# An attention and two feed-forward stages on one core: w3 kept as float32, lower parts of weights on VectorE, and two edits of order in the first attention steps

## Chip, cores and metric

The kernel runs on one core of one Trainium2 chip. The metric is the device time of one execution in microseconds. The time before is the median of three runs, 943.5 us (942.43 to 948.34).

## The reference

All arrays are float32. Attention has 4 batches of 8 heads, 576 positions and 64 columns; two feed-forward stages follow on 2304 tokens of width 512.

```python
scores = scale * np.matmul(q, k.transpose(0, 1, 3, 2))
cum = np.cumsum(np.maximum(s, 0.0), axis=-1)
bias = -(cum[:, :, :, None] - cum[:, :, None, :])
scores = np.where(causal, -1e9, scores + np.minimum(bias, 0.0))
attn = softmax(scores)
x = (attn @ v)                  # to (2304, 512)
h = x @ w_in                    # 512 -> 2048
x = (h - np.tanh(h)) @ w_out    # 2048 -> 512
a, b = x @ w1, x @ w2           # 512 -> 1024 each
out = ((a * b) @ w3) @ w_out2   # 1024 -> 1024 -> 512
```

## The kernel before

**Numbers in two parts.** Large products are made from float32 operands cut in two: `hi` is a cast to the format fp32r, `lo` the rest, `src - hi`, in the same format. A product takes three matmuls (hi hi, hi lo, lo hi; `mm3`, L113). `split` (L63) makes both parts: the cast by ACT (L64), the subtraction by POOL unless `lo` names another engine (L65). Weights arrive in another bit layout; `plain` (L84) puts them in order with three DVE instructions (L88, L91, L93) from the tile `raw` into `cvt`, two buffers each, and `convert` (L97) is `plain` and `split`.

**Order of the work.** TensorE's order is the order of the program. The instructions of all other engines, and SP's DMA issues, are put in order by a scheduler that simulates the kernel; each engine then takes its queue in that order, and an instruction that waits holds all behind it. `in_turn(i, behind)` (L80) orders `i` after `behind` on the same engine without a semaphore; `after_pe` adds a real wait.

**Stage 1 (0 to some 425 us): attention and the first half of the first feed-forward.** 32 pairs of heads go through a list of steps. `at(step, order, fn, p)` (L491) enters a function at a step; within a step functions run by `order`. Kind A is the first 256 positions of a pair of heads, kind B the other 320 in three units B1, B2, B3. The first eight pairs are batch 0 (`first`): four A, then four B. For a pair that begins at step k0, a unit's scores (PE) stand at its step k, `minimum` (DVE) and `exps` (ACT) at k+1, `transposes` (PE) and `evacuate` (the copy pf from PSUM, ACT) `lag` steps later, `products` (PE, the tile pv), then `invert`, `turn`, `store` (ACT copies rt, a DMA writes it), `spread` (two DMAs rb broadcast the reciprocals) and `finish` (L360): DVE multiplies pv by rb into `xy`, ordered behind `least[0]`, the last minimum that the program has so far. For the first four pairs `finish` stands at k0 + 10, `products` at k0 + 7. Their pv tiles take turns in two PSUM banks (L317), so pair 3's pv needs the bank that `finish` of pair 1 frees. Scores and transposes share five PSUM tiles `s` (`ps_a`); a tile comes free with the copy or the exponential that reads it. Small matmuls `spare` fill TensorE up to step 11.

The feed-forward generator `ffn` (L400) fills TensorE between attention steps, in nine blocks of 256 tokens. A block starts when `written` says that its rows are in `xy`; `cut_x` (L407) casts and subtracts the block's four column groups into `xhl`. `step_of` (L539 to L546) spreads the products of a block over the steps between its `avail` and that of the blocks after it. Beside this run `conversions` (L369), which makes the eight first groups of w_in and w_out (16 conversions, named win and wout), and from step 36 on `parked` (L383), which converts the other 16, and writes them to DRAM (`park`, L103, L106).

**Stage 2 (to some 622 us): the second half of that feed-forward** in blocks of 512 tokens, products hb and yb. Beside it `preparations` (L656) converts w1, w2, the second w_out and w3. Of w3's eight groups 6 and 7 stay on chip as hi and lo; six are written as hi and lo, 1 MB each, to `w3_d` (L688).

**Stage 3 (622 to 672 us): w3 times the second w_out,** eight groups of 24 products w3o in the order 6, 7, 4, 5, 0, 1, 2, 3 (L835). `fetch_w3` (L828) reads a parked group back into one of two buffers `park`. The loop also makes the operands of stage 4 (`need`, `weights`) and issues the first loads of its weights, S and A (`load_unit`, L782).

**Stage 4:** the products of w1, w2 and of the combined weights, in units of 384 columns.

Of the kernel before, what the change touches and what calls it, by code (L numbers as in the profile page):

```python
# [8 lines left out]
F32 = mybir.dt.float32  # L9
F32R = mybir.dt.float32r  # L10
BF16 = mybir.dt.bfloat16
U32 = mybir.dt.uint32
# [3 lines left out]
P = 128  # L16
# [3 lines left out]
DM = 512  # L20
# [3 lines left out]
NG = 8  # L24
BLK = 256
# [12 lines left out]
def tile_kernel(ctx: ExitStack, tc: tile.TileContext, qk, v, s, w_in, w_out, w1, w2, w3t, w_o2, outT):  # L38
    nc = tc.nc
# [12 lines left out]

    cum_d = dr.tile([NH, S], F32, tag="cum_d", name="cum_d")
    yp_d = dr.tile([P, NC, NT], F32, tag="yp_d", name="yp_d")
    w3_d = dr.tile([NG, P, 2, 2, DM], F32, tag="w3_d", name="w3_d")
    wf_d = dr.tile([2 * (NF - F1), P, 2, DM], F32, tag="wf_d", name="wf_d")
    wg_d = dr.tile([NG, P, 7, 2, 2 * P], F32, tag="wg_d", name="wg_d")
    wo_d = dr.tile([7, 2, P, 2, 2, 2 * P], F32, tag="wo_d", name="wo_d")
# [4 lines left out]
    def split(dst_hi, dst_lo, src, hi=None, lo=None):  # L63
        i = (hi or nc.scalar.copy)(dst_hi, src)  # L64
        (lo or nc.gpsimd.tensor_sub)(dst_lo, src, dst_hi.bitcast(F32))  # L65
        return i
# [30 lines left out]
    def convert(raw, name, w=None, lo=None, behind=None):  # L97
        t = plain(raw, name, behind)
        w = slot(name) if w is None else w
        split(w[:, 0, :], w[:, 1, :], t, lo=lo)  # L100
        return w

    def park(raw, name, dst, pool, behind):  # L103

        w = convert(raw, name, pool.tile([P, 2, DM], F32R, tag="park", name=f"park_{name}", bufs=1), behind=behind)
        nc.sync.dma_start(dst, w.bitcast(F32))  # L106

    def fetch(name, src):
# [14 lines left out]
    with ExitStack() as actx:  # L123
# [18 lines left out]

        REL = ((0, 0), (0, P), (1, 0), (1, 384), (0, 384))

        latest, least, last_exp, paces = [None], [None], [None], []
        PACED = 70

        def paced(i):
# [157 lines left out]
        def evacuate(p, j, e):  # L306
            pieces, pt, at = p.pf[j, e]

            pf = a2.tile([P, {"B1": 512, "B2": 416}.get(j, 384)], F32, tag=f"pf{0 if j == 'A' else j[1]}".replace("3", "0"), name=f"pf{p.n}_{j}_{e}")
            (nc.vector.tensor_copy if j == "B2" and not p.first else nc.scalar.copy)(pf[:, :at], pt[:, :at])  # L310
            p.pf[j, e] = pieces, pf, at

        def products(p, j):
# [55 lines left out]
        def conversions(fs):  # L369
            todo = [(d, f, src[f], f"{n}{f}") for f in fs for d, src, n in ((win, w_in, "win"), (wout, w_out, "wout"))]  # L370
            raws = []
            for m in range(2):
                raws.append(load_raw(*todo[m][2:], behind=latest[0]))
                yield
            for m, (d, f, src, n) in enumerate(todo):
                d[f] = convert(raws.pop(0), n, behind=least[0])
                if m + 2 < len(todo):
                    raws.append(load_raw(*todo[m + 2][2:], behind=latest[0]))
                yield
# [20 lines left out]
        def ffn():  # L400
            pend = []
            cut = {}

            def ready(blk):
                return blk < NB and all(written[b] >= min(S, (blk + 1) * BLK - S * b) for b in range(B))

            def cut_x(blk, lo):  # L407
                xs = cut.setdefault(blk, [])
                c, c0 = len(xs), blk * BLK
                x = f2.tile([P, 2, BLK], F32R, tag="xhl", name=f"xhl{blk}_{c}", bufs=6)  # L410
                split(x[:, 0, :], x[:, 1, :], xy[:, c, c0:c0 + BLK], lo=lo)
                xs.append(x)

            for blk in range(NB):
                c0 = blk * BLK
                while not ready(blk):
                    yield False
                while len(cut.get(blk, ())) < NC:
                    cut_x(blk, nc.vector.tensor_sub)
                xs = cut[blk]  # L420
                ys = []

                def add_y(f, gh, gl, end, ys=ys, blk=blk):
                    while f not in wout:
                        next(conv)
                    if f == 0:
                        ys.extend(ps_y.tile([P, 2, BLK], F32, tag=f"y{z}", name=f"y{z}_{blk}") for z in range(2))
                    for n, (z, x) in enumerate(((0, gh), (1, gh), (0, gl))):
                        for c in range(NC):
                            o = ys[c // 2][:, c % 2, :]  # L430
                            nc.tensor.matmul(o, wout[f][:, z, P * c:P * c + P], x,  # L431
                                             start=f == 0 and n == 0 and c % 2 == 0, stop=f == F1 - 1 and n == 2,
                                             skip_group_check=True)
                            if n == 1 and c == 1:
                                yield True
                    if f == F1 - 1:
                        after[1].append(end)

                def end_y(ys=ys, blk=blk, c0=c0):
                    for z in range(2):  # L440
                        yo = f2.tile([P, 2, BLK], F32R, tag="xhl", name=f"yo{z}_{blk}", bufs=6).bitcast(F32)
                        nc.scalar.copy(yo, ys[z])
                        nc.sync.dma_start(yp_d[:, 2 * z:2 * z + 2, c0:c0 + BLK], yo)

                for f in range(F1):
                    while f not in win:
                        next(conv)
                    late = written[B - 1] == S
                    ph = ps_a.tile([P, 512], F32, tag="s", name=f"h{blk}_{f}") if late else ps_h.tile([P, 512], F32, tag="h", name=f"h{blk}_{f}")
                    hh = ph[:, :BLK]  # L450
                    for c in range(NC):
                        pace[0] = mm3(hh, win[f], P * c, xs[c][:, 0, :], xs[c][:, 1, :], c == 0, c == NC - 1)
                        if c == 1:
                            yield True
                    t = f2.tile([P, BLK], F32, tag="th", name=f"th{blk}_{f}")
                    gh = f2.tile([P, BLK], F32R, tag="gh", name=f"gh{blk}_{f}", bufs=3)
                    gl = f2.tile([P, BLK], F32R, tag="gl", name=f"gl{blk}_{f}", bufs=3)

                    def tanh(t=t, hh=hh):
                        nc.scalar.activation(t, hh, AF.Tanh)  # L460

                    def rest(t=t, hh=hh, gh=gh, gl=gl, blk=blk):
                        nc.vector.tensor_sub(t, hh, t)  # L463
                        if blk < 2:
                            split(gh, gl, t)
                        else:
                            split(gh, gl, t, hi=nc.vector.tensor_copy, lo=nc.vector.tensor_sub)

                    after[0].append(tanh)
                    after[1].append(rest)  # L470
                    yield True
                    if len(pend) > late:
                        yield from pend.pop(0)
                    pend.append(add_y(f, gh, gl, end_y))
                    if f >= 3 and ready(blk + 1) and len(cut.get(blk + 1, ())) < NC:
                        cut_x(blk + 1, nc.vector.tensor_sub)
                    if blk == NB - 1 and f:
                        next(conv2, None)
                        next(conv2, None)
                    yield True  # L480
            for p in pend:
                yield from p
            yield True
            yield True
# [18 lines left out]
        for p in pairs:  # L503
# [18 lines left out]
            at(ke + 5, 2.4, turn, p)  # L522
            at(ke + 6, 1.2, store, p)
            at(ke + 6, 3.9, spread, p)
            fin = ke + lag + (5 if p.first and p.early else 3)
            at(fin, 2.6, finish, p)
            if p.hp == H // 2 - 1:
                avail.append((S * p.b + (BLK if p.early else S), fin))
# [122 lines left out]
    def load_w3(f, z):  # L651
        return load_raw(w3t[f, :, 4 * z:4 * z + 4].rearrange("p m c -> p (m c)"), f"w3_{f}_{z}", behind=pace[0])
# [3 lines left out]
    def preparations():  # L656
# [19 lines left out]
        for f in range(NG):  # L676
            if f == NG // 2:
                for m in range(NG):
                    convert(load_raw(w_o2[m], f"wo2_{m}", behind=pace[0]), f"wo2_{m}", wo2[m], lo=nc.vector.tensor_sub)
                    yield  # L680
            pk = wt.tile([P, 2, 2, DM], F32R, tag="park", name=f"w3p{f}", bufs=2)
            for z in range(2):
                convert(load_w3(f, z), f"w3_{f}_{z}", pk[:, z], lo=nc.vector.tensor_sub)
                yield
            if f in W3ORDER[:2]:
                kept[f] = pk
            else:
                nc.sync.dma_start(w3_d[f], pk.bitcast(F32))  # L688

    with ExitStack() as bctx:  # L690
        b2 = bctx.enter_context(tc.tile_pool(name="b2", bufs=2, reuse_waits="tile"))
# [135 lines left out]

    def fetch_w3(f):  # L828
        if f not in w3b:
            w3b[f] = wt.tile([P, 2, 2, DM], F32R, tag="park", name=f"w3b{f}", bufs=2)  # L830
            nc.sync.dma_start(w3b[f].bitcast(F32), w3_d[f])
        return w3b[f]

    ctx.enter_context(tc.manual_schedule(engines={mybir.EngineType.PE}))
# [221 lines left out]
```

## Time and profile before

| | |
|---|---|
| median of 3 runs | 943.5 us (942.43 to 948.34) |
| profiled execution | 942.7 us |
| its span, first to last instruction | 940.9 us |
| busy: PE, DVE, ACT, POOL | 914.4, 641.4, 452.6, 211.7 us |
| mean granted clock of TensorE | 0.995 |

The profile shows one execution. PE is TensorE's matmuls, PEld its weight loads, DVE VectorE, ACT ScalarE, POOL GpSimd, SP the engine that issues the DMAs. A tile is named by the program's name without its number, and Lnnn is the line. In a timeline a line has its start, its length, the engine, the line, the operation, the tiles and shapes, and in brackets the idle time of the engine just before and what ended it. The granted clock is a share of full speed: 1.00 is 2.4 GHz, 0.50 is 1.2 GHz.

### The profile page before, as it was taken

Reading aid. Unit: us, or ns where it says so; the run is one execution under the profiler, and the core shown is the slowest. Engines: PE = TensorE matmul, PEld = TensorE weight load, DVE = VectorE, ACT = ScalarE, POOL = GpSimd, SP = SyncE. Lnnn points to the kernel's source line nnn. Section 1 sums busy time; section 2 is a strip of 40 time slices with the busy share of each in tenths; the row PEclk is TensorE's granted clock in tenths of the full one; section 3 lists DMA queues with packets and bytes.
Section 4 is the critical chain, followed back from the end, with each engine's and each line's share of the span. In section 5 each row is a group of like instructions: output and inputs, shape, how many; then the busy total and the mean of one; then the engine's idle time right before and its main releaser. Section 6 shows DMA issues by size and latency. Waiting matters only on the chain.

```text
span 940.9 us, 16373 instructions
## 1 busy us (share of the span) xinstructions
PE 914.4 (97%) x6022; PEld 800.3 (85%) x6025; DVE 641.4 (68%) x1403; ACT 452.6 (48%) x1061; POOL 211.7 (22%) x210
## 2 busy tenths in 40 slices
PE   8889999899999999999999999998999999999998
PEld 4567777788888889998888888987899999999998
DVE  7677777787777866776999978763145747564555
ACT  4567887777776753323434433342123432433133
POOL 2245856666555410000000000000011111111100
PEclk9799999999999999999999999999999999999999
DMA  5655365535454423489687736258399877777774
GB/s 161 196 164 170 114 205 182 168 137 179 154 169 147 152 98 100 169 308 405 250 293 279 265 110 209 85 207 291 119 319 325 322 257 271 262 271 258 284 267 148
DMA packets 59072, 199.21 MB, mean 212 GB/s; under 512 B 6544, under 2 KB 21040, under 8 KB 53360
## 3 DMA queue, kind: packets, MB, share of 16 engines
q1 hardware_dynamic: 58992, 198.17, 60.8%
q8 instruction: 47, 0.77, 0.3%
q14 instruction: 33, 0.27, 0.1%
HBM read 151.86 MB, written 46.29 MB: 211 GB/s over the span
## 4 chain that ended last, share of the span: by engine, by line
PE 81%; DMA 7%; DVE 5%; ACT 3%; issue 2%; POOL 1%; SPq 1%; ACTq 0%; DVEq 0%; POOLq 0%
PE hb L117 10%; PE yb L117 10%; PE h L117 9%; PE W L861 9%; PE y L431 9%; PE oW L924 5%; PE Y L861 5%; PE s_B L229 4%; PE pv L327 4%; PE oY L924 4%; PE pt_B L301 3%; PE w3o L117 2%; DMA w3b<-w_d 2%; PE V L861 2%; DMA cb<-cum_d 2%
## 5 line engine op out<-in xcount | busy, mean ns | idle before, releaser
L117 PE MATMUL h<-xhl,win 128*128 128x256 f32 x864 | 120.6, 286 | 2.8 <-DVE xhl L65 1.9
L117 PEld LDWEIGHTS h<-xhl,win 128*128 128x128 f32 x864 | 105.8, 188 | 13.4 <-issue 4.3
L994 POOL TENSOR_TENSOR xy<-c,c 128x384 f32<-128x384 f32 x12 | 15.4, 1280 | 425.4 <-DVE c L983 425.4
L117 PE MATMUL hb<-x,win 128*128 128x512 f32 (+1 forms) x480 | 104.9, 367 | 0.0
L117 PEld LDWEIGHTS hb<-x,win 128*128 128x128 f32 x480 | 83.9, 188 | 15.0
L206 POOL TENSOR_SCALAR pr<-cb,cq 128x384 f32<-128x384 f32 (+1 forms) x48 | 90.8, 1904 | 22.8 <-DMA cb<-cum_d 14.3
L117 PE MATMUL yb<-ghb,wout 128*128 128x512 f32 (+1 forms) x320 | 95.6, 367 | 0.0
L431 PE MATMUL y<-gh,wout 128*128 128x256 f32 x576 | 85.2, 287 | 0.5 <-DVE gh L64 0.5
L290 ACT ACTIVATE pr<-pr,nm 128x128 f32<-128x128 f32 (+2 forms) x120 | 71.5, 598 | 19.0 <-DVE nm L268 18.9
L431 PEld LDWEIGHTS y<-gh,wout 128*128 128x128 f32 x576 | 72.5, 189 | 3.7 <-issue 2.0
L117 PEld LDWEIGHTS yb<-ghb,wout 128*128 128x128 f32 x320 | 58.2, 188 | 9.9
L117 PE MATMUL yb<-glb,wout 128*128 128x512 f32 (+1 forms) x160 | 58.4, 367 | 0.0
L301 PE MATMUL pt_B<-ident,pr 96*128 96x96 f32 (+1 forms) x384 | 51.4, 256 | 1.4 <-DVE cq L601 0.9
L268 DVE CUSTOM_DVE_ANT_0 pr<-s_B,pr 96x512 f32<-96x512 f32 (+1 forms) x72 | 44.1, 638 | 8.7 <-PE s_B L229 8.7
L431 PE MATMUL y<-gl,wout 128*128 128x256 f32 x288 | 45.1, 279 | 3.2 <-POOL gl L65 2.7
L301 PEld LDWEIGHTS pt_B<-ident,pr 96*128 96x128 f32 (+1 forms) x384 | 41.2, 143 | 5.7 <-issue 3.3
L463 DVE TENSOR_TENSOR th<-h,th 128x256 f32<-128x256 f32 x72 | 30.0, 417 | 22.3 <-ACT th L460 21.6
L310 ACT COPY pf_B<-pt_B 128x512 f32<-128x512 f32 (+2 forms) x72 | 35.8, 499 | 19.3 <-PE pt_B L301 19.3
L460 ACT ACTIVATE th<-h 128x256 f32<-128x256 f32 x72 | 26.8, 373 | 34.4 <-PE h L117 34.3
L872 ACT COPY s<-Y 128x384 f32<-128x384 f32 x24 | 11.6, 482 | 63.0 <-PE Y L861 60.5
L431 PEld LDWEIGHTS y<-gl,wout 128*128 128x128 f32 x288 | 38.3, 188 | 3.8 <-POOL gl L65 3.1
L64 ACT CAST ghb<-thb 128x512 fp32r<-128x512 f32 (+1 forms) x40 | 23.2, 579 | 35.2 <-DVE thb L725 34.5
(215 smaller groups left out, 2076.7 us busy)
## 6 DMA issues: line engine op xcount, KB each, us to landing
S<-wg_d SPq DMA_DIRECT2D x24, 1024.0 KB
wo<-wo_d SPq DMA_DIRECT2D x42, 512.0 KB
A<-wg_d SPq DMA_DIRECT2D x24, 768.0 KB
qk<-in_qk SPq DMA_DIRECT2D x16, 576.0 KB
raw_win<-in_w_in SPq DMA_DIRECT2D x16, 512.0 KB
raw_wout<-in_w_out SPq DMA_DIRECT2D x16, 512.0 KB
raw_w<-in_w SPq DMA_DIRECT2D x16, 512.0 KB
wg_d<-pks SPq DMA_DIRECT2D x8, 1024.0 KB
```

The source lines that it names most:

```text
L117: i = nc.tensor.matmul(ps, a, b, start=first and n == 0, stop=last and n == 2, skip_group_check=skip)
L206: nc.gpsimd.tensor_scalar(out=t[:pw, e, :w], in0=p.cb[:pw, e, :w], scalar1=c, scalar2=0.0, op0=ALU.add, op1=ALU.min)
L229: latest[0] = nc.tensor.matmul(ps[e][:PW[i], o:o + k1 - k0], w[r, 0, CH0[i]:CH0[i] + PW[i]], x[r, 1, k0:k1], start=z == 0 and (not p.first ...
L268: least[0] = nc.vector.tensor_tensor_reduce(out=t[:pw, k0:k1], in0=ps[:pw, o:o + k1 - k0], in1=t[:pw, k0:k1], scale=-0.125, scalar=nm[:pw, ...
L290: last_exp[0] = nc.scalar.activation(t[:pw, :], t[:pw, :], AF.Exp, bias=m, scale=-1.0, accum_out=p.sums[:pw, e, c:c + 1])
L301: nc.tensor.transpose(pt[:, at:at + pw], p.pr[i][:pw, e, KC0[kj]:KC0[kj] + P], ident[:pw, :pw])
L310: (nc.vector.tensor_copy if j == "B2" and not p.first else nc.scalar.copy)(pf[:, :at], pt[:, :at])
L327: nc.tensor.matmul(p.pv[D * e:D * e + D, c:p.nq], p.vs[:, e, kj], pf[:, beg:end], start=z == 0, stop=z == len(todo) - 1, skip_group_check= ...
L431: nc.tensor.matmul(o, wout[f][:, z, P * c:P * c + P], x, start=f == 0 and n == 0 and c % 2 == 0, stop=f == F1 - 1 and n == 2, skip_group_c ...
L463: nc.vector.tensor_sub(t, hh, t)
L861: i = nc.tensor.matmul(ps[:, :T], w[:, x, P * j:P * j + P], b[:, y, j], start=first and j == n == 0, stop=stop and j == 1 and n == 2, skip ...
L924: nc.tensor.matmul(ps[:, :T], w[:, a, q % 2, P * j:P * j + P], x[:, b, q], start=o in ("B11", "B21", "T1") and q == z == 0, stop=o in ("T4 ...
```

## The change

Four edits. (1) `w3_d` holds w3 in float32, half as large; a parked group is stored straight from the tile `cvt` and split when it is fetched, through a buffer `raw`. (2) `conversions` and `park` make the lower part on DVE; POOL made it before. (3) `finish` of the first four pairs stands one step later, at k0 + 11; `avail`, from which the first block's start is taken, moves with it. (4) The casts of the first block's `xhl` are ordered, on ACT, behind the last `evacuate` of a pair of batch 0 that the program has by then.

```diff
-    w3_d = dr.tile([NG, P, 2, 2, DM], F32, tag="w3_d", name="w3_d")
+    w3_d = dr.tile([NG, P, 2, DM], F32, tag="w3_d", name="w3_d")
...
     def park(raw, name, dst, pool, behind):
-        w = convert(raw, name, pool.tile([P, 2, DM], F32R, tag="park", name=f"park_{name}", bufs=1), behind=behind)
+        w = convert(raw, name, pool.tile([P, 2, DM], F32R, tag="park", name=f"park_{name}", bufs=1), lo=nc.vector.tensor_sub, behind=behind)
         nc.sync.dma_start(dst, w.bitcast(F32))
...
         def evacuate(p, j, e):
-            (nc.vector.tensor_copy if j == "B2" and not p.first else nc.scalar.copy)(pf[:, :at], pt[:, :at])
+            i = (nc.vector.tensor_copy if j == "B2" and not p.first else nc.scalar.copy)(pf[:, :at], pt[:, :at])
+            if p.first:
+                copied[0] = i
...
         def conversions(fs):
-                d[f] = convert(raws.pop(0), n, behind=least[0])
+                d[f] = convert(raws.pop(0), n, lo=nc.vector.tensor_sub, behind=least[0])
...
             def cut_x(blk, lo):
-                split(x[:, 0, :], x[:, 1, :], xy[:, c, c0:c0 + BLK], lo=lo)
+                in_turn(split(x[:, 0, :], x[:, 1, :], xy[:, c, c0:c0 + BLK], lo=lo), None if blk else copied[0])
...
-            fin = ke + lag + (5 if p.first and p.early else 3)
+            fin = ke + lag + (6 if p.first and p.early else 3)
...
     def preparations():
-            pk = wt.tile([P, 2, 2, DM], F32R, tag="park", name=f"w3p{f}", bufs=2)
+            if f in W3ORDER[:2]:
+                kept[f] = wt.tile([P, 2, 2, DM], F32R, tag="park", name=f"w3p{f}", bufs=2)
             for z in range(2):
-                convert(load_w3(f, z), f"w3_{f}_{z}", pk[:, z], lo=nc.vector.tensor_sub)
+                if f in kept:
+                    convert(load_w3(f, z), f"w3_{f}_{z}", kept[f][:, z], lo=nc.vector.tensor_sub)
+                else:
+                    nc.sync.dma_start(w3_d[f, :, z], plain(load_w3(f, z), f"w3_{f}_{z}"))
                 yield
-            if f in W3ORDER[:2]:
-                kept[f] = pk
-            else:
-                nc.sync.dma_start(w3_d[f], pk.bitcast(F32))
...
     def fetch_w3(f):
         if f not in w3b:
+            raw = cv.tile([P, 2 * DM], U32, tag="raw", name=f"raw_w3b{f}").bitcast(F32).rearrange("p (z c) -> p z c", z=2)
+            nc.sync.dma_start(raw, w3_d[f])
             w3b[f] = wt.tile([P, 2, 2, DM], F32R, tag="park", name=f"w3b{f}", bufs=2)
-            nc.sync.dma_start(w3b[f].bitcast(F32), w3_d[f])
+            split(w3b[f][:, :, 0], w3b[f][:, :, 1], raw, lo=nc.vector.tensor_sub)
```

## Rows read from the trace of the kernel before

**Rows 1.** Stretches of all engines: length, busy us (instructions), clock, DMA share, GB/s.
```profile
0.00:180.00 180.00, 165.04 (x1230) 119.76 (x1234) 131.26 (x358) 123.15 (x357) 95.46 (x106) 0.97 0.51 163
180.00:420.00 240.00, 238.11 (x2082) 210.94 (x2081) 178.32 (x515) 144.34 (x383) 85.14 (x81) 1.00 0.49 164
420.00:620.00 200.00, 200.00 (x991) 170.01 (x990) 160.32 (x292) 79.39 (x140) 0.00 (x0) 1.00 0.64 230
622.00:672.00 50.00, 44.84 (x197) 36.02 (x196) 22.16 (x30) 14.12 (x22) 0.00 (x0) 1.00 0.71 268
```

**Rows 2.** Waits of PE in the whole span: us, times, longest.
```profile
PE w3o L117 <- DMA w3b<-w_d: 5.2, 4, 2.8
PE y L431 <- POOL gl L65: 2.7, 2, 1.8
PE s_B L229 <- ACT rt L343: 2.5, 1, 2.5
```

**Rows 3.** Timeline of PE, 31 to 54 us.
```profile
31.37 0.55 PE L301 MATMUL pt_A<-ident,pr 128*128 128x128 f32 x3
34.42 2.28 PE L229 MATMUL s_B<-qk 64*128 64x384 f32 x8 [2.51 <-ACT rt L343]
...
38.37 1.55 PE L327 MATMUL pv<-pf_A,vs 128*64 128x256 f32 x8
...
50.48 0.51 PE L117 MATMUL h<-xhl,win 128*128 128x256 f32 x2 [1.43 <-DVE xhl L65]
...
51.27 1.06 PE L229 MATMUL s_B<-qk 64*128 64x384 f32 x8
...
53.10 0.21 PE L245 MATMUL s_B<-maskb,identb 128*96 128x64 bf16 x1
```

**Rows 4.** Timeline of ACT, 32 to 35 us.
```profile
32.06 0.41 ACT L64 CAST xhl<-xy 128x256 fp32r<-128x256 f32 x1 [3.52 <-DVE xy L364]
...
34.12 0.25 ACT L343 COPY rt<-pri 4x128 f32<-4x128 f32 x1
```

**Rows 5.** Timeline of DVE, 31 to 55 us.
```profile
31.61 0.43 DVE L364 TENSOR_TENSOR xy<-pv,rb 128x256 f32<-128x256 f32 x1 [2.30 <-DMA rb<-rd]
...
33.48 1.49 DVE L65 TENSOR_TENSOR xhl<-xy,xhl 128x256 fp32r<-128x256 f32 x1
...
54.65 0.16 DVE L261 TENSOR_SCALAR nm<-nm 96x2 f32<-96x2 f32 x1
```

**Rows 6.** Stretches around the low clock, columns as in rows 1.
```profile
0.00:34.40 34.40, 29.26 (x173) 16.06 (x176) 25.21 (x68) 15.70 (x55) 8.71 (x22) 1.00 0.57 170
34.40:44.60 10.20, 10.18 (x37) 6.30 (x38) 6.65 (x17) 4.67 (x16) 2.45 (x3) 0.50 0.59 200
44.60:60.00 15.40, 13.40 (x93) 9.71 (x92) 12.72 (x31) 10.25 (x30) 5.25 (x5) 1.00 0.60 190
```

**Rows 7.** Chain that ended last: start, us, what.
```profile
657.66 8.75 DMA w3b<-w_d
```

**Rows 8.** Timeline of all engines in the W3 stage.
```profile
621.04 0.68 SPq L789 DMA_DIRECT2D A<-wg_d  x1
...
660.48 5.72 PE L117 MATMUL w3o<-wo,w3b 128*128 128x512 f32 x24 [2.85 <-DMA w3b<-w_d]
```

**Rows 9.** Groups by line and shape: busy, mean ns, idle before and its releaser.
```profile
L206 POOL TENSOR_SCALAR pr<-cb,cq 96x512 f32<-96x512 f32 x24 | 50.2, 2100 | 0.0
...
L65 DVE TENSOR_TENSOR w3p<-cvt_w,w3p 128x512 fp32r<-128x512 f32 x16 | 10.9, 686 | 2.5 <-ACT w3p L64 2.4
...
L65 DVE TENSOR_TENSOR pks<-cs,pks 128x1024 fp32r<-128x1024 f32 x8 | 9.8, 1219 | 1.2 <-ACT pks L64 1.2
...
L64 ACT CAST pks<-cs 128x1024 fp32r<-128x1024 f32 x8 | 8.4, 1054 | 8.1 <-DVE cs L666 8.0
```

**Rows 10.** Timeline of POOL.
```profile
33.36 1.33 POOL L65 TENSOR_TENSOR win<-cvt_win,win 128x512 fp32r<-128x512 f32 x1 [7.86 <-ACT win L64]
...
164.52 1.93 POOL L65 TENSOR_TENSOR park_wout<-cvt_wout,park_wout 128x512 fp32r<-128x512 f32 x1 [4.94 <-ACT park_wout L64]
```

More of the change, by code (lines that the diff above doesn't have):

```diff
@@ L143, in tile_kernel @@
         REL = ((0, 0), (0, P), (1, 0), (1, 384), (0, 384))
-        latest, least, last_exp, paces = [None], [None], [None], []
+        latest, least, last_exp, copied, paces = [None], [None], [None], [None], []
         PACED = 70
```

## The prediction

> **What bounds the kernel now.** I read three views, from coarse to fine. First the stretches [rows 1]: TensorE (PE) is busy for 165.0 of the first 180 us, 238.1 of the next 240, 200.0 of 200 from 420 to 620, and 44.8 of 50 from 622 to 672, where W3 is multiplied. So the kernel is bound by TensorE, and only what ends a wait of TensorE, or raises its clock, counts: 15.0 us are idle before 180 us and 5.2 us in the W3 stage; VectorE (DVE) has 48.7 us idle before 180 us. Second, who ended TensorE's waits [rows 2]: the reload of w3b 5.2 us in four waits, gl made by GpSimd (POOL) 2.7 us in two, and one wait of 2.5 us for the copy rt by ScalarE (ACT). Third, the instructions around the waits. In the PE timeline [rows 3] pt_A ends at 31.92, and the scores s_B start only at 34.42, released by rt. The ACT timeline says why rt was late [rows 4]: a cast of xhl stood 3.52 us at the head of ACT for xy, made by DVE, and rt was behind it. The DVE timeline says why xy was late [rows 5]: the product with the spread reciprocals stood 2.30 us at the head of DVE for the transfer rb, and wrote at 31.61. After this stall the clock goes [rows 6]: from 34.4 to 44.6 us the granted clock is 0.50, TensorE's lower level of 1.2 GHz, where it was 1.00 before and is 1.00 after. The stall is paid twice, as wait and as half speed.
>
> In the W3 stage the chain [rows 7] shows a load of w3b that needs 8.75 us from issue to landing, the last of six. A reload is issued when the product two groups earlier has freed its buffer, so it has one group of products, 5.72 us [rows 8], to hide under; what is left over shows at 660.48, where TensorE stood 2.85 us for the load before the last one.
>
> **Part 1, W3 as float32.** The six parked groups are stored once, 512 KB each where hi and lo were 1 MB, and come back through the two raw buffers; then ACT casts and DVE subtracts. The nearest operations have the same 128x1024, the pair on pks: cast 1.05 us, subtraction 1.22 us [rows 9], 2.27 together. The buffer of the split frees as today, so 2.27 us must fit into 5.72: 3.4 us to spare. The load itself has a buffer of its own, free once the split two groups earlier is through: 2 x 5.72 - 2.27 = 9.2 us before its split is due, against 8.75 for twice the bytes. The first two can be issued before the stage begins, since the conversions have left the raw buffers by then. So the loads are hidden and the splits too; ACT and DVE are busy for 14.1 and 22.2 of the 50 us [rows 1] and get 6.3 and 7.3 more. I take -4.7 of the 5.2, with 0.5 left for a split that stands behind another cast. Bounds: -5.2, if all goes; +8.4, if all six splits were bare (6 x 2.27 - 5.2), far off, since 3.4 us of slack stand before each.
>
> The parking side loses 12 casts and 12 subtractions of 0.69 us [rows 9] between 420 and 620 us, at nothing: TensorE has no gap there. The cover also holds against the new dependence, a converted tile that is freed only when its store has landed: the same buffer is wanted two conversions later, and the landing of 1 MB took 8.75 us [rows 7]. Were the cover gone, DVE would stand in front of the tanh differences for that long; TensorE has two groups in hand before it notices. On SP six stores become twelve, behind other producers of the same step.
>
> **Part 2, the first four products a step on, and the casts behind copies.** The product of pair 1 is now issued behind the minimum of the next scores and no longer stands in front of it; the casts of the first block come after copies from PSUM, so rt and the pf copies no longer wait for xy. The 2.51 us go, and s_B starts at 31.9. What is late next: pair 3's pv uses the PSUM bank of pair 1's, so it must wait for that very product, which now follows the minimum of these scores. From the next pair's rows at full clock: s_B from 51.27 to 53.31, 2.04 us [rows 3]; its minimum ends at 54.81, 1.50 us behind [rows 5]; the product takes 0.43. So s_B ends at 33.9 and pv starts at 35.9, against 38.37 now: -2.4, with a new wait of 2.0 us. If the clock stays at 1.00, the 6.2 us from 38.4 to 44.6 that run at 0.50 shrink by half: -3.1. Together -5.5. Given back: four casts and subtractions of xhl, spread out so far, come in a row right before the first h. Today h waits 1.43 us there [rows 3]; I add 0.9, between nothing and twice 0.9. I take -4.6. Bounds: -6.9 if that wait goes too (5.5 + 1.4), and +0.5 if the clock falls all the same (first rival). Both bounds hinge on the clock: a wait of 1.43 us did not lower it, one of 2.51 did [rows 3, 6]; 2.0 lies between, and I lean to the shorter one since TensorE works on both sides of it. The start of the first block a step later spreads the same products over fewer steps: nothing.
>
> **Part 3, lower parts by VectorE.** 32 subtractions leave POOL, 1.33 us each [rows 10], and come to DVE at 0.69 [rows 9], each directly behind a cast by ACT; the like ones on w3p waited 2.5 us in 16, 0.16 each. After 180 us TensorE is busy for 238.1 of 240 and hides them. About 21 run before that, 16 of the conversions and some five parked: 21 x 0.85 = 17.9 us, into 48.7 us of idle DVE. What DVE holds up meanwhile are minima, tanh differences, and through them exponentials and copies. As TensorE waits for somebody 15.0 of 180 us, 8%, I let 8% through: +1.4. Against it POOL: the park subtraction at 164.52 held POOL for 4.94 us of waiting plus 1.93 of work in front of the causal mask and the bias [rows 10], and gl, queued behind these, made the longer of the two gl waits; I take a quarter of the 2.7 us, 0.6. Net +0.8. Bounds: -2.7 if both gl waits go and DVE hides all, +17.9 if nothing is hidden.
>
> One row shows VectorE and GpSimd in each other's way: a subtraction of xhl took 1.49 us from 33.48 [rows 5], where 0.69 is the time of one twice as wide [rows 9], while POOL subtracted from 33.36 to 34.69 [rows 10]. The Trainium skill, "SBUF — State Buffer", section "Who interferes with whom", states that a VectorE instruction with two SBUF inputs contends with a GpSimd instruction that reads SBUF, and that the first to start holds the shared ports for its whole length. By that rule the trace agrees, and the moved subtractions, which have two such inputs, are exposed to POOL's bias instructions. From rows: a bias instruction takes 2.10 us [rows 9], half of it 1.05, and POOL is busy for 95 of the 180 us [rows 1], 0.53; the nine of the 21 that run beside the bias, after 85 us, would lose 9 x 0.53 x 1.05 = 5.0 us of DVE time, of which 8% is 0.4: 935.4 by the rule, 935.0 without it.
>
> **Sum.** The profiled execution took 942.7 us, 0.8 under the median of the runs. 942.7 - 4.7 - 4.6 + 0.8 = 934.2, and with the 0.8 for a median 935.0.
>
> **Rivals.** First, the clock falls in the new wait of pv. For: it fell after 2.51 us, and 2.0 is nearer to that than to 1.43. Against: TensorE works until 33.9. Ten us at half speed from 35.9 end 4.0 us later than today's, so part 2 gives -2.4 + 2.0 + 0.9 = +0.5 in place of -4.6: 940.1.
>
> Second, the gain of part 2 is hidden later: ahead of 180 us other engines set the pace, and TensorE only waits elsewhere. For: 15.0 us of idle from many releasers. Against: the loads follow TensorE's own scores, so they shift with it. 942.7 - 4.7 + 0.8 + 0.8 = 939.6.
>
> Third, the first w3 loads aren't early: SP issues the last of four loads of S and A at 621.0 [rows 8], 3.5 MB in all, and if the raw loads come behind them the first split is late by about what a reload costs now, 3.0 us: 938.0.
>
> Fourth, better: both gl waits go and DVE hides its work: 935.0 - 0.8 - 2.7 = 931.5.
>
> Fifth, slower: DVE is the bound before 180 us. Place: 17 to 180 us, each subtraction at the head of DVE's queue waiting for its cast with minima behind it. Price 0.85 each, 17.9 in all, of which 1.4 is counted. To bring the time above 943.5 it needs 8.5 + 1.4 = 9.9 of the 17.9: it decides from 55% exposed; all of it gives 951.5, with the clock's fall 956.6. Against: DVE is idle for 27% of that time.
>
> **How the numbers follow.** A measurement of this kernel can tell about 1%, 9.4 us, from no change: below 934.1 is faster, above 952.9 slower. My case 0.48, its own range 931 to 938.5, with 0.23 of it under 934.1; clock falls 0.16; hidden later 0.08; late loads 0.07; better 0.13; DVE 0.08, of it 0.05 over 952.9. Faster 0.23 + 0.13 = 0.36; slower 0.05; the rest 0.59. The range reaches down past the fourth case to 930 and up past the first to 943.
>
> **What would show it.** Right: no wait for w3b, raw loads issued before the first w3 product, split below 3 us; s_B of the first B pair starting at 32 with a wait of about 2 us ahead of pv; granted clock 1.00 between 34 and 45 us; POOL idle until the first gl. Wrong: a clock of 0.50 anywhere after 30 us; TensorE's idle before 180 us still near 15 with DVE its commonest releaser; waits of w3 products for the split.

## The result, and the profile after

| | before | after |
|---|---|---|
| median | 945.2 us (9 runs, 936.99 to 948.34) | 933.1 us (9 runs, 932.31 to 939.26) |
| profiled execution | 942.7 us | 932.9 us |
| its span, mean granted clock | 940.9 us, 0.995 | 931.1 us, 0.996 |

The ratio is 0.990 with an interval of 0.9867 to 0.9934: faster by about 1%, which is just what a measurement of this kernel can tell. The 933.1 us are 1.9 under the forecast of 935.0 and inside its range; as a ratio to the 943.5 us that the forecast went by, it is 0.991. The nine runs lie in two groups, five from 932.3 to 933.1 at a mean granted clock of 0.996 and four from 937.5 to 939.3 at 0.989. (Lines are 2 to 4 higher in the kernel after: L329 was L327, L366 was L364, L833 is the new load of raw_w3b.)

First the stretches of the kernel after; the columns are those of [rows 1]. The W3 stage begins 4.9 us sooner, so its stretch is cut from 612.

```profile
0.00:180.00 180.00, 165.85 (x1265) 121.10 (x1266) 140.73 (x390) 125.29 (x365) 69.84 (x85) 0.98 0.53 170
180.00:420.00 240.00, 239.45 (x2091) 212.74 (x2091) 181.79 (x527) 142.28 (x377) 69.91 (x70) 1.00 0.49 166
612.00:662.00 50.00, 50.00 (x247) 42.55 (x246) 30.59 (x39) 20.98 (x31) 0.00 (x0) 1.00 0.53 189
```

TensorE is full in the W3 stage, where it stood 5.2 us. Up to 180 us it is hardly fuller than before (165.9 against 165.0), though DVE took over 9.5 us of work and POOL lost 25.6. The waits of TensorE (us in total, times, longest), to be read beside [rows 2]:

```profile
PE h L117 <- DVE xhl L65: 3.2, 1, 3.2
PE y L433 <- POOL gl L65: 2.5, 2, 1.4
...
PE pv L329 <- DVE xy L366: 1.5, 1, 1.5
...
PE W L865 <- DMA A<-wg_d: 1.0, 1, 1.0
```

The waits for w3b and rt are gone. The longest wait for xhl is 3.2 us where it was 1.43 [rows 3], the forecast wait of pv is there with 1.5 us, and gl costs nearly what it did. The timeline of TensorE from 31 to 48 us, to set beside [rows 3]:

```profile
31.66 1.43 PE L229 MATMUL s_B<-qk 64*128 64x384 f32 x8
...
35.54 0.87 PE L329 MATMUL pv<-pf_A,vs 128*64 128x256 f32 x8 [1.48 <-DVE xy L366]
...
42.23 0.58 PE L301 MATMUL pt_B<-ident,pr 128*128 128x128 f32 x4 [0.61 <-ACT pr L287]
...
43.67 0.43 PE L117 MATMUL h<-xhl,win 128*128 128x256 f32 x1 [0.46 <-ACT xhl L64]
47.31 1.01 PE L117 MATMUL h<-xhl,win 128*128 128x256 f32 x3 [3.21 <-DVE xhl L65]
```

The scores s_B start at 31.66 without a wait and pv at 35.54, 2.8 us sooner than before. Then the first products h wait 3.67 us in two pieces. Before, they began without a wait, and only the last two of the first twelve waited, the 1.43 us of [rows 3] (the timeline of the kernel before):

```profile
47.17 0.94 PE L117 MATMUL h<-xhl,win 128*128 128x256 f32 x6
```

The stretches around the new wait show what the granted clock did:

```profile
42.00:43.60 1.60, 0.90 (x5) 0.52 (x5) 0.37 (x2) 1.60 (x7) 0.00 (x0) 1.00 0.95 382
43.60:47.30 3.70, 0.43 (x1) 0.19 (x1) 3.21 (x7) 1.89 (x6) 0.00 (x0) 0.54 0.07 26
47.30:50.60 3.30, 3.29 (x13) 2.63 (x15) 3.30 (x7) 1.33 (x4) 0.00 (x0) 0.50 0.88 317
50.60:60.00 9.40, 8.62 (x59) 5.93 (x57) 6.91 (x22) 5.91 (x20) 0.74 (x1) 0.99 0.52 163
```

Closer, around the fall:

```profile
43.60:43.80 0.20, 0.13 (x1) 0.13 (x1) 0.00 (x0) 0.20 (x2) 0.00 (x0) 1.00 0.47 184
43.90:44.10 0.20, 0.20 (x1) 0.00 (x0) 0.01 (x1) 0.20 (x2) 0.00 (x0) 0.50 0.12 46
```

The clock falls to 0.50, the level of 1.2 GHz, at 43.9 us, while the first of these products (43.67 to 44.10) is still on TensorE. So it does not fall in the long wait but as that begins, behind waits of 0.61 and 0.46 us. It stays low through the long wait and through 3.3 us of full work behind it. The old stall with its low clock [rows 6] was exchanged for another wait and another low stretch, 10 us later; that the wait brought the low clock isn't shown here. Why xhl was late stands in the chain that ended last, of which these are the pieces from 39 us on (start, us, what):

```profile
39.04 5.02 DMA raw_win<-in_w_in
44.09 0.43 DVE cvt_win L88
44.51 0.60 DVE cvt_wout L91
45.11 0.60 DVE cvt_win L91
45.72 0.60 DVE cvt_wout L93
46.32 0.60 DVE cvt_win L93
46.92 0.35 DVE xhl L65
...
47.31 1.44 PE h L117 x5
```

The conversion of a weight that isn't needed yet stands at the head of DVE: it waits for its load until 44.09, five instructions of two conversions follow, and only then comes the subtraction of xhl that TensorE needs. On ACT the four casts were through by 44.5 us:

```profile
43.20 1.33 ACT L64 CAST xhl<-xy 128x256 fp32r<-128x256 f32 x4
```

To see where the time went, I read the start of some pairs' pv in the PE timeline (pairs counted from 0), that of w3o, and the span:

| | before | after | gained so far |
|---|---|---|---|
| pv of pair 3 | 38.37 | 35.54 | 2.8 |
| pv of pair 4 | 60.34 | 59.75 | 0.6 |
| pv of pair 14 | 176.11 | 172.29 | 3.8 |
| pv of pair 31 | 366.04 | 360.61 | 5.4 |
| first w3o | 622.35 | 617.49 | 4.9 |
| end of the span | 940.9 | 931.1 | 9.8 |

The first 2.8 us are given back to 0.6 by pair 4; 4.3 come between there and the W3 stage; 4.9 come behind it.

### The profile page after: what moved, and what is told of

The parts are those of the page before. It is cut to its first block, busy times and chain, and to the rows that moved or that the text cites. A ratio compares the mean times of both kernels' runs of the same rounds, so it can differ in the third digit from the quotient of the medians.

```text
span 931.1 us, 16354 instructions
## 1 busy us (share of the span) xinstructions
PE 911.1 (98%) x6025; PEld 799.0 (86%) x6025; DVE 650.4 (70%) x1429; ACT 449.1 (48%) x1055; POOL 170.9 (18%) x178
## 4 chain that ended last, share of the span: by engine, by line
PE 85%; DVE 5%; DMA 4%; ACT 3%; POOL 2%; issue 1%; SPq 0%; ACTq 0%; DVEq 0%
PE h L117 10%; PE hb L117 10%; PE y L433 9%; PE yb L117 9%; PE W L865 9%; PE oW L928 5%; PE Y L865 5%; PE w3o L117 5%; PE pv L329 4%; PE s_B L229 4%; PE oY L928 4%; PE pt_B L301 3%; PE V L865 2%; POOL pr L206 1%; PE s_A L229 1%
## 5 line engine op out<-in xcount | busy, mean ns | idle before, releaser
L117 PEld LDWEIGHTS yb<-ghb,wout 128*128 128x128 f32 x320 | 58.2, 188 | 10.2 <-ACT ghb L64 0.3
L218 POOL TENSOR_SCALAR_AFFINE_SELECT pr<-pr 128x256 f32<-128x256 f32 (+2 forms) x60 | 28.6, 495 | 98.3 <-issue 79.7
```

What stands on the lines that cost most here:

```text
L117: i = nc.tensor.matmul(ps, a, b, start=first and n == 0, stop=last and n == 2, skip_group_check=skip)
L218: nc.gpsimd.affine_select(out=dg, in_=dg, pattern=[[0, 2], [-1, w - c]], compare_op=ALU.is_ge, fill=-8e9, base=0, channel_multiplier=1)
```

## Experiments

Every kernel is compared with the kernel before on the same chip.

### Each part alone

`e1_w3` is the kernel before with edit 1 only (w3 in float32).

> The kernel before with part 1 alone (w3 stored as float32, split when fetched). My theory: the four waits for w3b (5.2 us) go whole, nothing else moves, so about 5 us under the kernel before (ratio 0.9945), TensorE busy for 50.0 of 50 us in the W3 stage, no wait for w3b. Rival (the early part carries the change, and the W3 stage only looks better because the operands of the next stage are ready sooner): ratio 1.00, a new wait of 3 us or more at the first products behind W3.

Measured: 940.2 us, ratio 0.9949 (0.992 to 0.9979). The profile has no wait for w3b and keeps the stall for rt, 2.8 us. By the ratio part 1 is worth 4.8 us.

`e2_steps` is the kernel before with edits 3 and 4 only:

```diff
-                split(x[:, 0, :], x[:, 1, :], xy[:, c, c0:c0 + BLK], lo=lo)
+                in_turn(split(x[:, 0, :], x[:, 1, :], xy[:, c, c0:c0 + BLK], lo=lo), None if blk else copied[0])
...
-            fin = ke + lag + (5 if p.first and p.early else 3)
+            fin = ke + lag + (6 if p.first and p.early else 3)
```

> The kernel before with part 2 alone (finish of the first four pairs a step later and the first block's casts behind the copies). My theory: pair 3's pv comes 2 to 3 us earlier, but the first h then waits 2 us or more for xhl and the clock falls there, so that little is left at the first pv of the B pairs (0.5 to 1.5 us) and at the end: ratio 0.997 to 1.000. Rival (the 3.8 to 5 us that the changed kernel has gained by 200 us are the shifted steps' own): about 5 us less, ratio 0.9945.

Measured: 950.9 us, ratio 1.0066 (1.0034 to 1.0098): slower. The pv of pair 3 starts 2.6 us sooner, that of pair 4 5.8 us later, and that of pair 31 6.8 later. Three timelines of this kernel, of PE, DVE and POOL, and its stretch from 40 to 60 us (columns as above) show why:

```profile
47.69 1.01 PE L117 MATMUL h<-xhl,win 128*128 128x256 f32 x3 [4.10 <-DVE xhl L65]
```

```profile
44.47 0.43 DVE L88 TENSOR_SCALAR cvt_win<-raw_win 128x512 uint32<-128x512 uint32 x1 [2.58 <-DMA raw_win<-in_w_in]
...
47.22 3.25 DVE L65 TENSOR_TENSOR xhl<-xy,xhl 128x256 fp32r<-128x256 f32 x3
```

```profile
47.43 1.35 POOL L65 TENSOR_TENSOR wout<-cvt_wout,wout 128x512 fp32r<-128x512 f32 x1 [6.55 <-ACT wout L64]
48.74 1.45 POOL L65 TENSOR_TENSOR win<-cvt_win,win 128x512 fp32r<-128x512 f32 x1
```

```profile
40.00:60.00 20.00, 14.38 (x55) 8.72 (x53) 13.42 (x30) 9.57 (x31) 3.64 (x3) 0.63 0.46 159
```

The wait is that of the kernel after, longer: DVE stood 2.58 us for the load, and three subtractions of xhl took 3.25 us while POOL subtracted weights from 47.43 to 50.19; in the kernel after, with POOL idle there, the same three took 1.09 (46.84 us). The granted clock is 0.63 from 40 to 60 us where it was 0.88 before; here it falls inside the wait, 1.6 us after its start at 43.6. What part 2 removes at 31 us it loses again at 44.

`e3_lows` is the kernel before with edit 2 only (`lo=nc.vector.tensor_sub` in `conversions` and `park`).

> The kernel before with part 3 alone (32 lower parts by VectorE). My theory: the stall at 31.9 us and its clock fall stay, but the waits for gl shrink and pairs behind 100 us run closer together: 2 to 4 us less, ratio 0.996 to 0.998. Rival (VectorE is the bound before 180 us, and the late xhl of the changed kernel is its sign): no gain or up to 5 us more, ratio 1.000 to 1.005, with the first h waiting 3 us for xhl here too.

Measured: 939.2 us, ratio 0.9958 (0.9931 to 0.9984): 4.0 us faster by the ratio. The stall for rt stays (2.7 us), and so does the low clock, 0.86 from 20 to 40 us. The two gl waits are 2.6 us, as before. The gain comes behind 78 us: from there to 370 us TensorE is idle 3.3 us, against 8.3 before, and small waits for copies pf, xy, xhl and th are gone. One group of DVE up to 180 us, first of the kernel before, then of e3 (busy us, mean ns, idle before):

```profile
L65 DVE TENSOR_TENSOR xhl<-xy,xhl 128x256 fp32r<-128x256 f32 x12 | 9.4, 784 | 6.7 <-ACT xhl L64 6.7
```

```profile
L65 DVE TENSOR_TENSOR xhl<-xy,xhl 128x256 fp32r<-128x256 f32 x12 | 6.4, 531 | 5.0 <-ACT xhl L64 5.0
```

Nothing was edited in these instructions, and they are a third shorter without POOL's subtractions beside them. The Trainium skill's "SBUF — State Buffer", section "Who interferes with whom", says that a VectorE instruction with two SBUF inputs contends with a GpSimd instruction that reads SBUF; these rows agree, 784 against 531 ns.

The three ratios multiply to 0.9973, the change has 0.990: the parts aren't independent. Part 2, slower alone, must cost less where DVE makes the lower parts. Two kernels test that.

### Which parts part 2 needs, and what it is worth

`a4_convpool` is the changed kernel with the conversions' lower parts back on POOL:

```diff
-                d[f] = convert(raws.pop(0), n, lo=nc.vector.tensor_sub, behind=least[0])
+                d[f] = convert(raws.pop(0), n, behind=least[0])
```

> The changed kernel with the 16 conversions' lower parts on GpSimd again, the 16 parked ones on VectorE. My theory: parts 2 and 3 need each other in the conversions: GpSimd's subtractions hold VectorE's two-input instructions around 40 us, the first h waits 4 us for xhl as in the kernel with part 2 alone, and the clock falls for longer: 4 to 8 us over the changed kernel. Rival (the gain of part 3 is all from the parked ones, by shorter waits for gl): within 1.5 us of the changed kernel.

Measured: 940.2 us, ratio 0.9961 (0.9943 to 0.9979), by the ratios 6 us over the changed kernel. The first h waits 5.78 us; DVE stood 3.29 us for raw_win, and the three xhl took 3.25 us again beside POOL.

`b1_nosteps` is the kernel before with edits 1 and 2, without part 2.

> The kernel before with part 1 and part 3, without part 2 (the first four products keep their step, the casts their free order). Theory: what the two other parts give adds up, 0.9949 x 0.9958 = 0.991 of the kernel before, about 935.5 us, and part 2 is worth nothing measurable beside them, since its first h gives back at 44 to 50 us what the missing stall at 31 us saved; the profile then shows the stall of 2.5 us for rt, a granted clock under 0.9 between 30 and 50 us, no long wait of the first h, and no wait for w3b. Rival: part 2 pays as soon as the conversions' lower parts are VectorE's; then this kernel is about 4.6 us slower than the changed one, 0.995, 938 us.

Measured: 936.0 us, ratio 0.9899 (0.9863 to 0.9935), against 0.990 of the changed kernel. The wait for rt was 1.31 us in this profile, not 2.5, and yet the clock was 0.88 from 20 to 40 and 0.76 from 40 to 60 us. So beside the other two parts, part 2 makes no difference that these runs show.

`a3_nocast` is the changed kernel without edit 4.

> The changed kernel without the order of the first block's casts behind copies. My theory: the finish a step later is what keeps rt in time; without the order the casts spread out again, so the first h waits less: 0 to 4 us under the changed kernel. Rival (the casts' order is what takes the 2.5 us wait away): the wait of s_B for rt is back at 31.9 us with the clock's fall, 3 to 6 us over the changed kernel.

Measured: 935.0 us, ratio 0.9905 (0.9881 to 0.993). The later step alone shortens the wait for rt to 0.7 us; a wait of 2.29 us for a copy pf_B by ACT is at 48.18 us in place of that for xhl, and the clock is 0.72 from 40 to 60 us. The casts' order makes no difference that these runs show.

### The wait ahead of the first h

`a1_xhl_pool` gives the first block's lower parts to POOL, so that they pass DVE's queue by:

```diff
-                in_turn(split(x[:, 0, :], x[:, 1, :], xy[:, c, c0:c0 + BLK], lo=lo), None if blk else copied[0])
+                in_turn(split(x[:, 0, :], x[:, 1, :], xy[:, c, c0:c0 + BLK], lo=lo if blk else None), None if blk else copied[0])
```

> The changed kernel with the first block's four lower parts of xhl made by GpSimd, which has nothing else to do there. My theory: the wait of the first h (3.2 us, and 0.5 for the cast) shrinks to under 1.5 us, the granted clock stays 1.00 from 40 to 60 us, and the 3.2 us of wait and some 3 us of half speed come off: 4 to 6 us under the changed kernel, 927 to 929. Rival (what is gained before 60 us is only waited for before 180 us): 0 to 1 us under the changed kernel, with longer waits between 60 and 180 us.

Measured: 938.9 us, ratio 0.9942 (0.9919 to 0.9966), by the ratios 4 us over the changed kernel. The theory that this subtraction's place in DVE's queue is the whole cause fell. Rows of this kernel, from the timelines of PE, then ACT, then DVE:

```profile
45.10 1.68 PE L117 MATMUL h<-xhl,win 128*128 128x256 f32 x5 [0.48 <-POOL xhl L65]
...
50.46 2.06 PE L229 MATMUL s_B<-qk 64*128 64x384 f32 x8 [3.00 <-ACT pf_B L310]
```

```profile
48.78 0.62 ACT L64 CAST wout<-cvt_wout 128x512 fp32r<-128x512 f32 x1 [3.69 <-DVE cvt_wout L93]
```

```profile
44.91 0.43 DVE L88 TENSOR_SCALAR cvt_win<-raw_win 128x512 uint32<-128x512 uint32 x1 [1.98 <-DMA raw_win<-in_w_in]
45.25 1.22 DVE L91 SCALAR_TENSOR_TENSOR cvt_wout<-raw_wout,cvt_wout 128x512 uint32<-128x512 uint32 x1
```

The wait of h shrank to 0.94 us (0.46 and 0.48), and yet the clock fell, at 44.6 us, and is 0.61 from 40 to 60 us. Besides, a cast of a weight then stood at the head of ACT, behind the same late conversion, and held the copy pf_B: TensorE waited 3.00 us for that. POOL's subtractions (3.88 us from 44.31) also stretched the conversions, 1.22 us where the kernel after has 0.69. So it is the conversion that has to go from there.

`a5_hold` holds the conversions of steps 15 to 17 to step 18, in the loop that hands them to the steps:

```diff
-            if convs < 2 * F1 + 2 and k >= 1 + 2 * convs:
+            if convs < 2 * F1 + 2 and k >= 1 + 2 * convs and not 15 <= k <= 17:
```

> The changed kernel with the conversions of steps 15 to 17 held until step 18. My theory: in the changed kernel VectorE stands 1.7 us for the load of raw_win and then does four conversion instructions ahead of the xhl that the first h waits for; with the conversions behind it that wait falls from 3.2 us to 1 us or less, the granted clock stays 1.00 from 40 to 60 us, and the kernel comes to 927 to 929 us, ratio to the kernel before 0.982 to 0.985, with less spread between runs. Rival (as with xhl by GpSimd, the wait only moves to the next copy from PSUM, because ScalarE's casts of the conversions stand before it): no more than 1 us under the changed kernel, ratio 0.989 to 0.991, with a wait of 2 us or more between 44 and 60 us.

Measured: 931.8 us, ratio 0.987 (0.9848 to 0.9893), five runs from 929.8 to 932.8, all at a clock of 0.998. The TensorE timeline and the stretch from 40 to 60 us:

```profile
43.81 0.38 PE L117 MATMUL h<-xhl,win 128*128 128x256 f32 x1 [0.31 <-ACT xhl L64]
...
44.35 0.85 PE L117 MATMUL h<-xhl,win 128*128 128x256 f32 x5 [0.16 <-DVE xhl L65]
```

```profile
40.00:60.00 20.00, 18.17 (x120) 12.10 (x119) 17.44 (x42) 12.66 (x38) 0.74 (x1) 1.00 0.60 206
```

The wait is 0.47 us where it was 3.67. That shows the cause of the wait: with the conversion of win in another place it goes. From 40 to 60 us the clock is 1.00. But it fell elsewhere in this profile, from 36.7 to 40.1 us, behind the same wait of 1.48 us for pv that left it at 1.00 in the kernel after:

```profile
35.50:38.60 3.10, 2.92 (x13) 1.06 (x14) 2.08 (x6) 2.87 (x11) 0.00 (x0) 0.70 0.45 180
```

So the low stretch is shorter, 3.4 us where it was some 7, not gone. The pv of pair 4 comes 4.2 us sooner than in the kernel after, that of pair 14 only 2.0, so half is waited for elsewhere. The ratio lies between the 0.982 to 0.985 of my theory and the 0.989 to 0.991 of the rival.

`b2_hold_nocast` is the same without edit 4.

> The changed kernel without the casts' order, with the conversions of steps 15 to 17 held to step 18. Theory: the hold takes away the wait ahead of the first h whether or not the casts are ordered, and the product's later step alone takes away the stall for rt; so this comes out like the version with the order and the hold, 0.987, 931 to 932 us, with a granted clock above 0.95 between 40 and 60 us. Rival: without the order a cast of xhl stands ahead of rt or of a copy of pf again; then a wait of 2 us or more for ACT shows between 31 and 50 us, and the time is that of the changed kernel, 933 to 935 us.

Measured: 932.4 us, ratio 0.9879 (0.9843 to 0.9915), six runs from 930.8 to 934.7 at clocks of 0.998 and 1.00. The hold does it, with the casts' order or without. In this profile too the clock fell behind the wait for pv, at 35.5 us, and was 1.00 from 40 to 60 us.

`a7_hold_spare` is `a5_hold` with the small matmuls `spare` up to step 17 in place of 11.

> The changed kernel with the conversions held as before and the three spare matmuls kept up to step 17 (up to step 11 so far). My theory: they cost some 0.65 us a step where TensorE has work and nothing where it waits, and they keep the clock up through the wait for pv in every run: granted clock 0.998 or more in all runs, spread of the runs under 3 us, median within 1 us of the one with the conversions held alone. Rival (the clock does not fall there in any case, and the spare matmuls only cost): 2 to 4 us over the one with the conversions held alone.

Measured: 932.7 us, ratio 0.989 (0.9862 to 0.9918), six runs from 930.1 to 938.0 at clocks from 0.990 to 0.998. The spares didn't keep the clock up in every run; that theory fell.

The versions with the hold have the lowest medians, below both kernels. Against the changed one their intervals overlap; what can be told is that in eleven runs of `a5_hold` and `b2_hold_nocast` none was above 934.7, where four of nine of the changed kernel were above 937; of the six of `a7_hold_spare` one was, with 938.0.

## Why the prediction came out

The total was right, and two of its terms were not; they are off by +4.0 and -5.1 us and nearly cancel, so that the sum came out is luck. Two of the three signs of being wrong that the prediction named came true: a clock of 0.50 after 30 us, and 14.2 us of idle TensorE before 180 us with DVE as the commonest releaser (3.2 us for xhl, 1.5 for xy). By the table of starts:

| step | forecast | measured |
|---|---|---|
| part 1, W3 | -4.7 | -4.9 in the profile, -4.8 alone |
| part 2, up to pair 4 | -4.6 | -0.6 in the profile, +6.2 alone |
| part 3, pair 4 to W3 | +0.8 | -4.3 in the profile, -4.0 alone |
| sum | -8.5 | -9.8 |

**Part 1** held by its steps. The raw loads are issued ahead of S and A, and the splits have the lengths taken from the pair on pks (issues on SP's queue; then the groups on w3b with minimum, median and maximum ns):

```profile
596.92 1.01 SPq L833 DMA_DIRECT2D raw_w3b<-w_d  x1
...
603.22 0.33 SPq L833 DMA_DIRECT2D raw_w3b<-w_d  x1
...
614.86 0.32 SPq L789 DMA_DIRECT2D S<-wg_d  x1
```

```profile
L64 ACT CAST w3b<-raw_w3b x6: 1049/1051/1051, 624.3 to 650.8; 128x1024 fp32r<-128x1024 f32 x6
L65 DVE TENSOR_TENSOR w3b<-raw_w3b,w3b x6: 1219/1225/1226, 626.3 to 651.9; 128x1024 fp32r<-128x1024 f32 x6
```

The 5.2 us of waits went altogether, and 1.0 us for A is new behind them in this profile (0.2 in that of `e1_w3`). The third rival (loads late behind S and A) fell.

**Part 2.** The scores' start (31.9 forecast, 31.66 measured), the new wait of pv (2.0 and 1.48) and its start (35.9 and 35.54) came near what was worked out, and the clock didn't fall there in this profile. That is luck as well: of seven profiles with this wait (1.48 or 1.49 us) the clock stayed at 1.00 behind it in four, and fell in `a4_convpool`, `a5_hold` and `b2_hold_nocast`, as the first rival had it, though for some 3.4 us and not for ten. The step that failed is "four casts and subtractions of xhl, spread out so far, come in a row right before the first h. Today h waits 1.43 us there [rows 3]; I add 0.9". Already the reading was off: the 1.43 us stand ahead of the last two of the first twelve products, at 50.48, not ahead of the first. The row of casts was no trouble. What I left out is whatever else stood in DVE's queue between them: a conversion waiting for its load, and four more instructions of conversions behind it. The wait grew by 2.24 us (3.67 less 1.43). The clock fell as it began, which cost half of the 3.3 us at 0.50 behind it, 1.65; the prediction had taken it at 1.00 there. Together that is 3.9 us against the 0.9 that I added, a miss of 3.0 of the 4.0 us that the term is off. Of the other 1.0, 0.9 are further waits of TensorE between the pv of pair 3 and that of pair 4 (idle for 5.15 us there after, 1.99 before), the 0.61 us for pr among them. Alone this part is slower, so it even had the wrong sign where POOL keeps the subtractions.

**Part 3.** The step that failed is the net of "I let 8% through: +1.4" and "I take a quarter of the 2.7 us, 0.6". The moved subtractions themselves behaved as forecast, 683 ns on win and 752 on wout, with little waiting in front. But the gl waits didn't shrink, and the gain lies in what the sum had nowhere: DVE's own instructions beside POOL's subtractions get shorter (784 to 531 ns on xhl), and small waits of TensorE behind them go. DVE's busy time up to 180 us rose by 9.5 us for the 14.5 of work that came (21 times 0.69), although the kernel was 3.8 us ahead by then and had done that much more. The prediction knew the row, 1.49 us for a subtraction of xhl beside POOL [rows 5], and charged the effect to the moved instructions; it belonged on the other side of the account, as a gain of those that stay. That this contention is all of part 3's gain is argued from these durations, not shown by a kernel that changes nothing else.

**The rivals.** The second had the symptom, part 2's gain gone later, and its larger piece went by another mechanism than the pace of other engines, a conversion in DVE's queue: held conversions bring 4.2 us back at pair 4. But only 2.0 of these are left at pair 14, and beside parts 1 and 3 the whole of part 2 is worth nothing that the runs show; for that the rival isn't refuted. The fourth (gl waits go) fell, though its number, 931.5, was near. The fifth (DVE becomes the bound) fell as a price: DVE was idle for 39 us up to 180, and the kernel is faster with its added work.

## What to carry to other kernels

When instructions of a queue are moved, list everything that stands in that queue between the old and the new place, with the load that each waits for: work that isn't urgent, ahead of work that is, costs as much as its own load is late, and its own length besides. Where two engines stretch each other's instructions, moving work from one to the other can also pay on the instructions that stay, so sum both sides. Test parts of a change with and without each other: here one part was slower alone, and worth nothing measurable beside the rest.

## What the runs showed of the hardware

The length of a wait does not settle whether the clock falls. The same wait of 1.48 us, ahead of the same pv, left the clock at 1.00 in the kernel after, and not in `b2_hold_nocast`; the stretch behind it, first of the one and then of the other:

```profile
35.50:37.00 1.50, 1.46 (x12) 0.80 (x12) 0.78 (x3) 1.41 (x5) 0.00 (x0) 1.00 0.81 332
```

```profile
35.50:38.60 3.10, 3.09 (x12) 1.17 (x12) 2.14 (x6) 3.10 (x12) 0.00 (x0) 0.50 0.22 47
```

`b2_hold_nocast` has a wait of 0.82 us for rt some 3 us earlier, which the kernel after lacks; but `a3_nocast` has 0.74 us there and 1.49 for pv, and stayed at 1.00. Nor does the fall always come in the wait: in `a5_hold` it came 1.0 us behind its end, with TensorE at work, and in the kernel after behind waits of 0.61 and 0.46 us, as the long one began.

How long it stays low differs too: 3.4 us in `a5_hold`, about 7 in the kernel after, 10.2 before [rows 6], and some 20 in `e2_steps`, up to 65.6 us. With 0.50 as the only lower level, the mean clock of a run gives an estimate of the whole: 2 x 0.004 x 931 = 7 us for the mean of 0.996 of the profile after, as seen there. A mean of 0.989 is then some 20 us, 13 more, worth 6.5 us of full work. The eleven runs of `a5_hold` and `b2_hold_nocast`, at 0.998 or more, had at most 4 us. Which wait is hit in a run that wasn't profiled stays open.
